# Threshold attention into a maxout FFN: the softmax's 1/sum applied after the product with V instead of before it, with a new issue order

## The chip, the cores and the metric

The kernel runs on one core of one Trainium2 chip. The time is the device time of an execution in microseconds (us); of the kernel before there are three runs.

## The reference

There are 8 batches, 8 heads, 576 positions and a head size of 64. The output has 4608 rows of 512 float32. `randn` inputs stand in float32, tau is 0.02.

```python
scores = scale * np.matmul(q, k.transpose(0, 1, 3, 2))
thresh = np.max(scores, axis=-1, keepdims=True) - tau
scores = np.where(scores >= thresh, scores, -1000000000.0)
scores = scores - np.max(scores, axis=-1, keepdims=True)
attn = np.exp(scores)
attn = attn / (np.sum(attn, axis=-1, keepdims=True) + 1e-09)
x = np.matmul(attn, v)            # then heads side by side: 4608 x 512
h = np.maximum(np.maximum(x @ w1, x @ w2), x @ w3)   # 512 x 768 each
out = h @ w_out                                      # 768 x 512
```

## The kernel before, in words

**Tiling.** A batch has two quads of four heads, so there are 16 quads, `g` = 0 to 15. A quad's attention is cut into nine chunks of 128 partitions (query rows; a partition row holds one query row of one head), each with two halves `r` of 576 columns: 16 x 9 x 2 = 288 halves. Scores come out of float32 matmuls (`sc`) into a PSUM bank. `maximum` (DVE) copies a half to SBUF as `z` and takes its row maximum `nm`. `exponents` (ACT) and `numerators` then make the thresholded exponentials and their sum in one of these ways, chosen per half by a digit of `MASKED`:

- digits 1 and 3 ("masked"): ACT takes Exp, then DVE multiplies by the mask `z >= exp(-tau)` and sums (`SCALAR_TENSOR_TENSOR`);
- digits 0 and 2: ACT applies Prelu with the threshold and then Exp with a sum (two passes on ACT); with 0, DVE makes the threshold `th` first;
- digits 2 and 3 read the scores from PSUM in the first ACT pass instead of from `z`.

`reciprocals` (DVE) takes 1/sum of the two halves of a chunk, `normalized` (POOL) writes `P = z * 1/sum` as bfloat16, half by half, and `turned` sends P through a transposing DMA on SP's queue into `ptq`. When a quad's nine chunks are there, `product` multiplies with V on TensorE (`o`), and the result is evacuated into `xt`, for r = 0 by DVE, for r = 1 by ACT. When both quads of a batch are in `xt`, the FFN follows in pieces: 18 hidden pieces (`ph`; ACT evacuates the first of three, DVE takes the two maxima), then output pieces (`po`). Batch 7 is split in two parts of its rows (`SPLIT`), so there are 18 units of (quad, part) that pass through `product`.

**Order.** Nothing is scheduled at run time. `ORDER` is a string written out by hand or by a planner, one letter for each step, and `issue` carries the letters out; on every engine, and on SP's DMA queue, instructions run in that order. Letters that the text uses: S a half's scores, T transposes of q and k, O a product with V, F and B the two halves of an FFN piece, m maximum, s threshold, e first ACT pass, n second ACT pass, k masked product, r reciprocals, p the scaling on POOL, t the transposing DMA, w and x the evacuation of a product by DVE and by ACT, h and v the evacuations of hidden pieces, l loads of q, k and v, g loads of weights, z their casts on POOL, o and i stores. The digit behind S, T, O, F and N names the pair of PSUM banks, of which there are four.

**Buffers.** Nine z buffers, and from the 72nd half on two more that the weight stage lends (`MORE_Z`, `half_of_z`); six P buffers, two `stage` buffers.

**A reading aid.** All instructions carry the line of one helper (L93), so the profile tells them apart by the names of their tiles.

Of the kernel before, what the change touches and what calls it, by code (L numbers as in the profile page):

```python
# [15 lines left out]
OP = AluOpType  # L16
# [5 lines left out]
FLAT = 2.0 ** -100  # L22

MASKED = """
232222322322222222021032222202332122123122200200111000000000100000000011
000010111020011000101000000001100001001000010011111100000000100100000000
110010030111000100010000000001010100001110001011010100110000000000000000
100101101011000000120000001010000000110011100000001110001000010011111021
# [6 lines left out]
MORE_Z = 72  # L35
# [5 lines left out]
llllllglllT0laclT1laclzllqqS0qqS1meS2mS3lmlT0enlkS1ylmlT2eamelrnpS3leqlmnyS1qcapS0emtnrcS3pmnT2qmepgrelS1qya  # L41
gS0pmelT2mqnS3tcpemqS2nlkT1eytaS0rmnT1kpermS3yS2enczrmS1qT0enmepnqtS3nprmaymgpeS0lptS2mppT0mtpS1enencnqsS3re
rmtpS0mS1penmS3lqnsS2mtperpekzllmT0tmpenkT1pgS3eearnS0petmnqrS2meqlnpS3lmnplsS2cetpremS1pS0nmplermtzeS3mnS2p
mtnpmS3rkpS1leektS0emnrpmemptS1eekS2pO3mktS0rennmpermT2pnS1wptemS3prkyO0tmeakS2pgS1enxlnrmS0lpesS2mezT3mS1np
mgntspcS2eqrseT3mtpeS0srmapS1mnT2ptS3mnqO0ceqmeO1prswnptnkS3pxS0meF1meS2zBresmT0qghF3klpF2nkBtaS1sveS0pemF3B
nyrrsmyBepT1svS0hpcT2nS3zmaS1erpgsF2mntpsBmnS3yvF1etssT0myeBprS2cnpS3mnS0ympelF2epF3lmBnzslssvS0htBrqmeS2vpn
S1gF0sepmF3teqBmF2erssvpBtnBkphF0eS1vtS3znmF2nrBmqteS1rpvBnS3pmlnF0pmgeS1qsBsrhmS3pevS2npS1mF0npsO3ermpesmO2
zewepgsskBxtT3nF1vS2nklBarS0mlphS3mtepF2sS1rmnyBmetF3pvT0eBpcnS2tzT1nvS0asmzS3temS2qeS1meF0trkpmS3lenpBmnlys
reklpF1umerpskS3upBeoketmS0uS2umpS3tesmS1qeT0myO2nqlrsnlprcO3etqsmepwS0xptS1mnF3psnmS2BlerskpS1thF0meF3pmeBF
2ktnBveBsrS1nvpS0hmyF3emF2npBrssT0eprtvBaF1kS3nqvBeF0myhyS2kyleF3mBelBvnpS2snsS0vptemS1pnF3rmpT2tnBmpeF0scS1  # L50
htBrnmpF3erT2rpvlBasS1pstvnS2pmeF0pS3emtBqnmT2S1hcqS3empF2eS0rsqmtS1epsmBeF3pmnF0stsvBeBknF2klhF1BvelS0nrvpB
emT3pS2arvS0ptnS3mpnO1smtesrkpeF2swnlrpmeT0S1qtescS3epBmnpmnT0trskS3paS1umS0ulqmeS3lmyS1nopS2smelS0rmeS3psmn
O1ypersmqO2etkpemO0lewqxlknpS3tS1keF2momS3lexF0ktT1enkBercpnsBpumN1ertkphkF3jS0rursS1empBnmF2ptS0vpS1smeF3yt
BsnsmBpnvS0pT1hmF2atT3srepS0cF1eprBsmeqF3vnByBynvplS2nsS0plmhS1mteS2mF0nF3mteS1rrspBnmS2pelvBlepF1smT0leqBvl
aS2rkhF3oqnsS0mtS1epmBeqsF2ssmtS0epvBeyF1mnF3vpBesrS0ktphBermS1npT2svO0nytmpncT3eS1wF2nrmS0aBrsmnqF3vnT1pS0c
eBptsF2mhpS1eS3pmteS0qmBeO1spmnkteF3rvnpT0BsskapS2xvS0erS1qmtnS3pmnF2mqlespmeS1rtkBepresmT3puS1cuS0ptmnS3pS2
meyS1lrekpF0tnsmempO3lekteskO2nrsmpeBkpxrnwS1uptS3muS2pnmF0yoeS1mF3lesymBtnS2srkpS1hmBeF0spveF2ertBmpT3nrsvS
1paBlmpnS0tS3qhmF1epsmS2leBymF3tevF0nBknlS1rsvpS2esmqnBF3srmhpS1epS0tmeF2pssBrempBtesvS0ynF1mT3lnpBvF0lhsrcS
2tnT1mBnF3valS2nrBsqmeF0pvS1epS2meBptsmS3eqF1hmT2peBcS3tnskT2O0arkplnmO2lerpvewptS3xkpS1nF2meF0sstreBsmpS3nv
pBnmS1tS2hmT3eF0rmpnF1cBpnBrevptT3S2apvS0qmtS3S1enmqF2esrsqmiepmleS0soykeS1plBnmemtS3ukS0uT1snrlO2cpekynO1me  # L60
ymeF3pwxskteS0keS1BrrnkopmF2pmS0BqeuurtsmF1phS3srnpS2meT0ptBmeS3ykpaN2esvempF0tS1jkpF3ermBeS2ptvnS1pmBnS0rls
hsmpS2elF3mqntS1mpF0nsrBskpeF2lsmBetBpveF1yhvS3lnkS2lesF0mytnBmBerqsS3veF2lpvnF1pBsmT0htBceF3rT2vnpBsaS0pvnF
1qmtS2nBsrnmT0pS3hrcpF2esS1mpteS0rmpS3emBpntF1svqnS0ssBmpeoT2vO3lamtneF1wS0nrlBpmeS3qsrS2hsmS0pnmF1eptS3smeB
pmF2ntS0veS3rsmnpS1BnpO0veytrempS2empS3xsmS1tekF0nsknlT2rmpBelmlpnscS3quS1umyS2eorT0kpeO3tmeyO1ewlepsmF3etka
rknS2qklT0nBmxespcS2eryF0mpF1uskpuBtnS2BhmqF3nsvS0peS2srmtpF1eBmpeF0srvnBptS2hyS3pmeF1lmeBlBevtF3nkT2S0arrvp
BnS2mphS1smpF0ntS3smnpBmeF1lsT2esvlF3nrBrcptBnvpS2eS0qmlhS1tsnprsmT3F2epmS0aptBemF3yevS1oS0nqmBnpsrS2mnF1ptv
S0epmBeS3mthS2skeF0F1snmlBeklO3ersvpnrmByepF0swT2eqtBvnqF3ssrcS1hpiBmpT0S2vaptS1snmS0pnT3mqF2tecT1BarmS3pnS1
vqeS0mF2pesrmnptmS3npT1seS0qctBeymqermpS1eS3mpuF0nmtuskS1eS2klnS3smBesrsepO1upmemO2txrkpukeO3wnkpS0xS2emF3et
rmS1pnBssspmF2hS0rtepS3mnBpmF1etS0veF3mnN2rnpBpjF0evtF2esBkBkhF1nsvS3eBmBevO3hrkS2pwnS1mnF3prmS2eptsF0mnBpsS
1sevyS2terBmpeF3svS1iyepBmoS0yhmtF2ekF3nBsmS1ersBvpnF0pmeF2BvteS1hBmF3rsS0vpeF1rknpBBmnO2vhptO0xrpnS3pwS2trm  # L70
npS0mnF3pmteF1pBeBvtS0rS2vpS3empF1ktkF0kBereskpemBkperumO2uptO3xpN1wtenkO2jrF3pxF1hpF2nvF3tvF1rhF2pvF3pvF1hF
2tvF3vF1hF2voF3vF1ohF2vF3vF1hF2vO3vO1wF2xuuF1oF0hiF3vF1vF0hF3vF1vF0hF3vF1vF0hF3vF1vF0hF3vF1vF0huF3vF1ovF3uoF
0uoN1fjdi
# [31 lines left out]
def kernel(  # L105
# [44 lines left out]
    def weight_loads():  # L150


        def piece(dst, src):
            my = {}

            def load():
                my["t"] = stage.tile([128, 4 * 256], F32, name="stage")
# [19 lines left out]
    small = ctx.enter_context(tc.tile_pool(name="small", bufs=6))  # L177
# [177 lines left out]
    halves_of_z = iter(range(1 << 20))  # L355

    def half_of_z():

        n = next(halves_of_z)
        if n >= MORE_Z and (n - MORE_Z) % (ZBUFS + 2) >= ZBUFS:  # L360
            return stage.tile([128, 4 * 256], F32, name="stage")[:, :S]
        return zz.tile([128, S], F32, name="z")

    def maximum(c, r):

        z = c["z", r] = half_of_z()
# [8 lines left out]
    def threshold(c, r):  # L375
        th = c["th", r] = small.tile([128, 1], F32, name="th", bufs=5)
        vector.tensor_scalar(out=th, in0=c["nm", r], scalar1=-1.0, scalar2=tau, op0=OP.mult, op1=OP.subtract)
# [452 lines left out]
```

## Time and profile before

| | |
|---|---|
| median of three runs | 446.92 us (446.69, 446.92, 449.09) |
| profiled execution, span from first to last instruction | 444.8 us; the median lies 2.1 us above it |
| granted TensorE clock, mean | 0.988 |
| DMA | 88.50 MB, 199 GB/s on average |
| scalings `P<-z,rs` and `P<-stage,rs` on POOL | 250 and 38 instructions |
| transposing DMAs `ptq<-P` | 144 |

"Busy" is the time in which an engine has at least one instruction running. Instructions of an engine overlap a little at their ends, so durations add up to more than the busy time. In the tables of windows each row is a stretch of the span, with the busy time of PE (matmuls), PEld (weight loads), DVE, ACT and POOL, then the granted clock, the mean share of the 16 DMA engines that were busy (overlapping packets can bring it over 1) and the rate in GB/s.

### The profile page before, as it was taken

The numbers are of one execution on the slowest core, as the hardware profiler recorded it, in microseconds if no ns is written. First come the engines' busy times: TensorE is split into PE (matmuls) and PEld (weight loads), VectorE is DVE, ScalarE is ACT, GpSimd is POOL, SyncE is SP. The second block draws the span as 40 slices with busy tenths as digits, with TensorE's granted clock in tenths as the row PEclk, the third lists the DMA queues.
The fourth block names the chain that finished last, engine by engine and source line by source line (L and its number), as shares of the span: only waits on it lengthen the run. The fifth ranks groups of instructions, "written<-read, shape, count | busy, mean of one in ns | idle before, by whom it ended". The sixth has DMA issues, their size and how long they took to land.

```text
span 444.8 us, 14254 instructions
## 1 busy us (share of the span) xinstructions
PE 422.4 (95%) x5188; PEld 320.2 (72%) x5190; DVE 392.8 (88%) x1228; ACT 403.0 (91%) x836; POOL 311.9 (70%) x420
## 2 busy tenths in 40 slices
PE   7767789999999999999999999999999999999996
PEld 6334347787788767787788777788688886787873
DVE  3887999999999999999999999998999998899642
ACT  3999999999999999999999999899999999987632
POOL 2799989997878687696785877676676685457400
PEclk8998999999999999999999999999999999999999
DMA  7999999999999999699899999989999977487633
GB/s 188 275 293 199 291 169 269 235 243 262 229 180 194 212 222 292 125 256 167 143 234 189 230 198 203 209 168 210 208 206 194 244 151 105 83 179 136 145 116 108
DMA packets 213959, 88.50 MB, mean 199 GB/s; under 512 B 189184, under 2 KB 202240, under 8 KB 213888
## 3 DMA queue, kind: packets, MB, share of 16 engines
q1 hardware_dynamic: 213360, 86.96, 95.9%
q8 instruction: 41, 0.67, 0.6%
q10 hardware_dynamic: 528, 0.62, 0.5%
q14 instruction: 30, 0.25, 0.2%
HBM read 35.65 MB, written 9.44 MB: 101 GB/s over the span
## 4 chain that ended last, share of the span: by engine, by line
PE 86%; ACT 5%; DVE 4%; issue 2%; DMA 1%; SPq 0%; DVEq 0%; ACTq 0%
PE ph L93 32%; PE sc L93 32%; PE po L93 10%; PE o L93 9%; ACT z L93 5%; PE tp L93 3%; DVE z L93 3%; DMA qm<-in_q_dram 1%; ACT qt L93 1%; SPq L93 0%; DVE xt L93 0%; DVE hm L93 0%; DVE stage L93 0%; DVE rs L93 0%; ACT ob L93 0%
## 5 line engine op out<-in xcount | busy, mean ns | idle before, releaser
L93 POOL TENSOR_SCALAR P<-z,rs 128x576 bf16<-128x576 f32 x250 | 200.6, 814 | 63.3 <-DVE rs L93 28.1
L93 DVE TENSOR_SCALAR_CACHE_REDUCE z<-sc 128x576 f32<-128x576 f32 x250 | 183.7, 750 | 14.8 <-PE sc L93 10.1
L93 PE MATMUL sc<-kt,qs 64*128 64x256 f32 (+2 forms) x640 | 182.6, 423 | 5.7 <-DVE z L93 2.3
L93 PE MATMUL sc<-kt,qt 64*128 64x320 f32 (+2 forms) x640 | 182.4, 433 | 5.2 <-ACT z L93 3.3
L93 PE MATMUL ph<-xt,w 64*128 64x288 bf16 (+2 forms) x2160 | 170.8, 283 | 0.1
L93 PEld LDWEIGHTS <-w 64*128 64x128 bf16 (+1 forms) x2160 | 130.1, 94 | 28.6 <-issue 4.3
L93 ACT ACTIVATE z<-z 128x576 f32<-128x576 f32 x174 | 117.6, 679 | 0.1
L93 PEld LDWEIGHTS sc<-kt,qs 64*128 64x128 f32 (+1 forms) x640 | 92.4, 180 | 25.7 <-DVE z L93 5.7
L93 ACT ACTIVATE z<-z,th 128x576 f32<-128x576 f32 x143 | 106.2, 769 | 5.0 <-DVE th L93 4.2
L93 PEld LDWEIGHTS sc<-kt,qt 64*128 64x128 f32 (+1 forms) x640 | 91.9, 179 | 19.7 <-ACT z L93 5.9
L93 DVE SCALAR_TENSOR_TENSOR z<-z 128x576 f32<-128x576 f32 x76 | 62.2, 830 | 0.5 <-ACT z L93 0.5
L93 PE MATMUL po<-wo,hT 64*128 64x512 bf16 (+3 forms) x454 | 53.5, 354 | 0.3
L93 POOL COPY qs<-qt 64x640 f32<-64x640 f32 (+3 forms) x66 | 43.0, 652 | 10.8 <-ACT qt L93 7.2
L93 ACT ACTIVATE z<-z,nm 128x576 f32<-128x576 f32 x68 | 50.6, 767 | 0.0
L93 DVE TENSOR_TENSOR hm<-ph,hm 128x576 bf16<-128x576 f32 (+2 forms) x54 | 37.0, 686 | 9.2 <-PE ph L93 8.9
L93 ACT ACTIVATE hm<-ph 128x576 bf16<-128x576 f32 (+2 forms) x54 | 31.8, 589 | 13.4 <-PE ph L93 12.8
L93 POOL TENSOR_SCALAR P<-stage,rs 128x576 bf16<-128x576 f32 x38 | 30.4, 804 | 19.3 <-ACT z L93 5.4
L93 PEld LDWEIGHTS <-hT 64*128 64x128 bf16 (+2 forms) x456 | 30.0, 95 | 16.5 <-issue 2.3
L93 DVE TENSOR_TENSOR hT<-ph,hm 128x576 bf16<-128x576 f32 (+2 forms) x54 | 37.0, 686 | 4.0 <-PE ph L93 2.3
L93 PE MATMUL o<-ptq,vb 128*64 128x64 bf16 (+2 forms) x544 | 39.0, 281 | 0.0
L93 ACT ACTIVATION_READ_ACCUMULATOR z<-z 128x1 f32 x174 | 34.3, 197 | 0.0
L93 PEld LDWEIGHTS <-vb 128*64 128x64 bf16 x544 | 23.3, 111 | 12.8 <-issue 4.9
(45 smaller groups left out, 431.6 us busy)
## 6 DMA issues: line engine op xcount, KB each, us to landing
vm<-in_v_dram SPq DMA_DIRECT2D x32, 256.0 KB, 4.8
qm<-in_q_dram SPq DMA_DIRECT2D x15, 512.0 KB, 5.0
km<-in_k_dram SPq DMA_DIRECT2D x15, 512.0 KB, 5.3
out_dram<-ob SPq DMA_DIRECT2D x14, 512.0 KB, 4.0
stage<-in_moe_w_dram SPq DMA_DIRECT2D x9, 512.0 KB, 5.2
ptq<-P SPq DMA_TRANSPOSE x144, 4.0
vr<-in_v_dram SPq DMA_DIRECT2D x16, 128.0 KB, 3.4
stage<-in_moe_w_out_dram SPq DMA_DIRECT2D x3, 512.0 KB, 4.9
```

What stands on the lines that cost most here:

```text
L93: ins = fn(*a, **kw)
```

## The change

P is no longer scaled. `numerators` writes bfloat16 P itself, from ACT's Exp or DVE's masked product, and the sums of a unit's chunks are gathered in one tile `sm` of 20 columns. When a unit's last sum is there, step r takes their reciprocals into `turn` and transposes it in blocks of 32 on DVE; step D (new) stores the result as rows in a DRAM tile; step R (new) loads the rows back with each row spread over 64 partitions, two DMAs for a unit, into a buffer of the weight stage. All evacuations of products are now on DVE and multiply by that tile. POOL's scalings and the letters p and x go; r falls from 144 to 18; D and R come, 18 each. In `MASKED`, 96 halves instead of 86 are masked, 14 instead of 8 of the first 36; no digit 4, which `by_pool` would read, stands in it. `ORDER` is new throughout. The z buffers that the stage lent are given up, and the ninth's output `ob9` uses a z buffer.

```diff
-MORE_Z = 72
...
+    rows = ctx.enter_context(tc.tile_pool(name="rows", bufs=2, space=bass.MemoryType.DRAM))
...
+    def half_of_p(c, r):
+        if "P" not in c:
+            c["P"] = pp.tile([128, W], BF16, name="P")
+        return c["P"][:, r * S:(r + 1) * S]
...
     def numerators(c, r):
-        z, acc = c["z", r], c["sm"][:, r:r + 1]
-        if masked(c["g"], c["idx"], r):
-            vector.scalar_tensor_tensor(out=z, in0=z, scalar=thr, in1=z,
+        z, p, acc = c["z", r], half_of_p(c, r), sum_of(c, r)
...
+        elif masked(c["g"], c["idx"], r):
+            vector.scalar_tensor_tensor(out=p, in0=z, scalar=thr, in1=z,
                                         op0=OP.is_ge, op1=OP.mult, accum_out=acc)
         else:
-            scalar.activation(out=z, in_=z, func=AF.Exp, scale=-1.0 / FLAT, accum_out=acc)
-
-    def reciprocals(c):
-        c["rs"] = small.tile([128, 2], F32, name="rs")
-        vector.reciprocal(c["rs"], c["sm"])
-
-    def normalized(c):
-        c["P"] = P = pp.tile([128, W], BF16, name="P")
-        for n in range(2):
-            pool.tensor_scalar(out=P[:, n * S:(n + 1) * S], in0=c["z", n],
-                                    scalar1=c["rs"][:, n:n + 1], scalar2=1.0, op0=OP.mult, op1=OP.mult)
...
+            scalar.activation(out=p, in_=z, func=AF.Exp, scale=-1.0 / FLAT, accum_out=acc)
...
+    turns = [one.tile([128, 2, 32], F32, name=f"turn{x}") for x in range(2)]
+
+    def reciprocals(g, part, n):
+        L, t = Ls[g], turns[n % 2]
...
+        if part is None:
+            vector.reciprocal(new[:, :, f:f + 9], sums[:, :, f:f + 9])
...
+            vector.reciprocal(new[to, :, at:at + 1], sums[of, :, was:was + 1])
+        vector.transpose(t[:, 1, :], t[:, 0, :])
+        scales[g, part] = dict(t=t)
+
+    def scale_rows(g, part):
+        s = scales[g, part]
+        s["rows"] = rows.tile([32, 128], F32, name="rows")
+        sync.dma_start(out=s["rows"].rearrange("j (b t) -> b j t", b=4), in_=s["t"][:, 1, :])
+
+    def scale_tile(g, part):
+        s, (lo, hi) = scales[g, part], span(part)
+        n = hi - lo
+        s["R"] = stage.tile([128, W], F32, name="stage").rearrange("p (r n) -> p r n", r=2)[:, :, 0:n]
+        src = s["rows"].rearrange("j t -> (j t)")[0:2560].rearrange("(r i y) -> i r y", i=2, y=640)
+        o = 64 * ninth_first(Ls[g]["b"]) + lo
+        for i in range(2):
+            sync.dma_start(out=s["R"][64 * i:64 * i + 64],
+                           in_=src[i, :, o:o + n].unsqueeze(0).to_broadcast([64, 2, n]))
...
-        def on_vector():
...
-            vector.tensor_copy(out=dst[:, lo:hi], in_=ps[:, base:base + hi - lo])
-        def on_scalar():
...
-            scalar.activation(out=dst[:, lo:hi], in_=ps[:, base:base + hi - lo], func=AF.Copy)
+        def done():
+            ps = st["ps"]
+            dst = target(L["b"])[:, 2 * L["qd"] + r, :]
+            vector.tensor_tensor(out=dst[:, lo:hi], in0=ps[:, base:base + hi - lo],
+                                 in1=scales[2 * L["b"] + L["qd"], part]["R"][:, r, :], op=OP.mult)
...
-                ob = hp_.tile([128, DM], F32, name="ob9", bufs=1)
+                ob = zz.tile([128, S], F32, name="z")[:, 0:DM]
```

More of the change, by code (lines that the diff above doesn't have):

```diff
@@ L641 @@
     number = {x: n for n, x in enumerate(steps)}
-    Ls, xts, stores, stores9, ends, ninths = {}, {}, [], [], [], []
+    Ls, xts, stores, stores9, ends, ninths, scales = {}, {}, [], [], [], [], {}
     def x_of(b):
@@ L663 @@
     vector.memset(vrs[2], 0.0)
+    for t in turns:
+        vector.memset(t[:, 0], 1.0)
     for t in vrs[0:2]:
@@ L697, in products, with units @@
                         yield product(Ls[g], r, x_of, part)
+    def units():
+        n = 0
+        for b in range(B):
+            for part in parts_of(b):
+                for g in (2 * b, 2 * b + 1):
+                    yield g, part, n
+                    n += 1
     def flow(what, fn):
@@ L732, in issue @@
             p.first(where)
[L733 to L735 removed]
+            line["w"].append(p.evac)
         elif what in "FN":
@@ L758, in issue @@
             line["k" if masked(c["g"], c["idx"], r) else "n"].append((c, r))
-        elif what in "nk":
-            c, r = line[what].pop(0)
-            if "sm" not in c:
-                c["sm"] = small.tile([128, 2], F32, name="sm")
-            else:
-                c["summed"] = True
-            numerators(c, r)
-        elif what == "r":
-            c = made[line["r"].append(0) or len(line["r"]) - 1]
-            assert c["summed"]
-            reciprocals(c)
-            line["p"].append(c)
+        elif what in "nkX":
+            numerators(*line[what].pop(0))
+        elif what == "r":
+            g, part, n = next(todo["r"])
+            reciprocals(g, part, n)
+            line["D"].append((g, part))
+        elif what == "D":
+            g, part = line["D"].pop(0)
+            scale_rows(g, part)
+            line["R"].append((g, part))
+        elif what == "R":
+            scale_tile(*line["R"].pop(0))
         elif what == "t":
```

154 lines of the change are left out of this document (89 added, 65 removed).

## The prediction

> **What bounds the kernel now.** I read the page's busy table first, then a table of windows, then the groups kept apart by shape, and last the timelines of single engines and of SP's queue.
>
> ```profile
> span 444.8 us, 14254 instructions
> PE 422.4 (95%) x5188; PEld 320.2 (72%) x5190; DVE 392.8 (88%) x1228; ACT 403.0 (91%) x836; POOL 311.9 (70%) x420
> 25.00:50.00 25.00, 18.24 (x128) 10.49 (x128) 20.06 (x63) 23.89 (x54) 24.00 (x33) 0.86 1.13 248
> 50.00:75.00 25.00, 21.51 (x235) 12.67 (x235) 24.84 (x77) 24.75 (x53) 21.96 (x27) 1.00 1.10 232
> 75.00:100.00 25.00, 24.94 (x333) 20.59 (x330) 24.17 (x80) 25.00 (x57) 23.67 (x33) 1.00 1.13 238
> 100.00:125.00 25.00, 25.00 (x308) 19.43 (x309) 23.61 (x75) 24.83 (x51) 20.95 (x27) 1.00 1.13 225
> ```
>
> The columns of the windows are PE, PEld, DVE, ACT, POOL busy, granted clock, DMA share and GB/s. From 75 us on PE is busy for 24.94 and 25.00 of 25 us: from there the kernel is TensorE's, and the change takes no matmul away. Before 75 us PE idles; ACT is full (24.75 of 25) and DVE too (24.84). So a gain can only come from an earlier start of the dense part, and a loss from anything that holes it. The start of the dense part is the first `ph`:
>
> ```profile
> 69.39 1.18 PE L93 MATMUL o<-ptq,vb 128*64 128x512 bf16 x16
> 73.06 0.67 PE L93 MATMUL ph<-xt,w 64*128 64x288 bf16 x8
> 120.36 1.22 PE L93 MATMUL o<-ptq,vb 128*64 128x512 bf16 x15
> 124.10 0.66 PE L93 MATMUL ph<-xt,w 64*128 64x288 bf16 x8
> ```
>
> The product of the second quad of batch 0 runs at 69.39 and the first hidden piece at 73.06; for batch 1 the same pair is at 120.36 and 124.10. Both products need the last transpose of their quad, so SP's queue is the second thing to read.
>
> ```profile
> 56.25 10.68 SPq L93 DMA_TRANSPOSE ptq<-P  x5
> 104.52 1.44 SPq L93 DMA_DIRECT2D vm<-in_v_dram  x2
> 106.00 9.90 SPq L93 DMA_TRANSPOSE ptq<-P  x5
> L93 SPq DMA_TRANSPOSE ptq<-P x144: 1241/1432/4678, 17.6 to 418.9; - x144
> DMA packets 70760, 28.80 MB, mean 230 GB/s; under 512 B 61254, under 2 KB 67398, under 8 KB 70739
> ptq<-P SPq DMA_TRANSPOSE x40, 4.9
> ```
>
> Five transposes fill SP for 10.68 us, five for 9.90 us: 2.1 and 2.0 us each, where the shortest takes 1241 ns. The 28.80 MB row is the window 25:150, the row x40 (4.9 us to landing) the window 50:150. SP has no holes here and the DMA share stands at 1.10 to 1.13: in the first 150 us the queue is as full as ACT. The transposes of batch 1 end at 115.90, landing 4.9 makes 120.8, and the products start at 120.36. Nothing is in reserve there.
>
> **The change part by part.** The rows that price it:
>
> ```profile
> L93 POOL TENSOR_SCALAR P<-z,rs 128x576 bf16<-128x576 f32 x250 | 200.6, 814 | 63.3 <-DVE rs L93 28.1 <-ACT z L93 11.6 <-DVE th L93 7.4
> L93 DVE SCALAR_TENSOR_TENSOR z<-z 128x576 f32<-128x576 f32 x76 | 62.2, 830 | 0.5 <-ACT z L93 0.5
> L93 DVE RECIPROCAL rs<-sm 128x2 f32<-128x2 f32 x144 | 22.0, 157 | 2.0 <-ACT z L93 1.4 <-ACT stage L93 0.2
> L93 DVE TENSOR_TENSOR hm<-ph,hm 128x576 bf16<-128x576 f32 x42 | 31.5, 751 | 0.8 <-PE ph L93 0.6
> L93 DVE CAST xt<-o 128x576 bf16<-128x576 f32 x14 | 10.5, 749 | 0.5 <-PE o L93 0.5
> L93 ACT ACTIVATE xt<-o 128x576 bf16<-128x576 f32 x14 | 9.0, 640 | 0.2
> 402.46 0.67 ACT L93 ACTIVATE z<-z 128x576 f32<-128x576 f32 x1
> 403.12 0.67 ACT L93 ACTIVATE stage<-stage 128x576 f32<-128x576 f32 x1
> 403.79 0.76 ACT L93 ACTIVATE stage<-stage,nm 128x576 f32<-128x576 f32 x1
> 408.27 0.75 DVE L93 SCALAR_TENSOR_TENSOR z<-z 128x576 f32<-128x576 f32 x1
> 408.95 0.75 DVE L93 SCALAR_TENSOR_TENSOR z<-z 128x576 f32<-128x576 f32 x1
> 409.63 0.15 DVE L93 RECIPROCAL rs<-sm 128x2 f32<-128x2 f32 x1
> 409.70 0.13 DVE L93 TENSOR_SCALAR th<-nm 128x1 f32<-128x1 f32 x1
> ```
>
> Durations overlap at their ends, so what an instruction costs its engine is the step from start to start: 0.66 us on ACT (402.46 to 403.12, and 403.12 to 403.79), 0.68 on DVE for a full half (408.27 to 408.95), 0.07 for a small one (409.63 to 409.70).
>
> *POOL.* All 288 scalings go: 200.6 us of this form alone. In the windows POOL is full only from 25 to 50 (24.00 of 25), and ACT is as full there, so this frees latency (a P is ready one or two passes of 0.81 us sooner) and no bound by itself.
>
> *ACT.* The masks hold 96 masked halves instead of 86: ten exponentials fewer, 10 x 0.66 = 6.6 us. The evacuations of x leave: 14 x 0.640 = 9.0, and four small ones. About 16 us of 403.0.
>
> *DVE.* 144 reciprocals go, 144 x 0.07 = 10 us; 18 groups of two to four reciprocals and a transpose of 128x32 come. That transpose has no row: between a small instruction (0.07) and a full half (0.68); with so few elements I take 0.15, so 18 x 0.35 = 6 us. Ten masked halves more: 10 x 0.68 = 6.8. Evacuations of x: 14 x 0.749 = 10.5, and four small ones, 12 us in all; the multiplication costs nothing over the cast by the row of `hm<-ph,hm` (751 against 749). On the other side, the masked product takes 830 ns on average, but 0.75 at 408.27 and 408.95, where POOL ran nothing; without POOL's scalings the 96 save up to 0.08 each, 7.7 us. Balance about +7 us on 392.8. The Trainium skill says why, in "SBUF — State Buffer", section "Who interferes with whom": a VectorE instruction with two SBUF inputs contends with a GpSimd instruction that reads SBUF. By that rule the 7.7 us come in full, and the rows agree.
>
> *The front.* Counted in the two orders up to the first hidden piece, before to after: Prelu or Exp of the first pass 50 to 47, second-pass exponentials 37 to 29, masked products 12 to 16, maxima 53 to 52, evacuations of x on ACT 2 to 0, on DVE 2 to 4. With the steps above and the evacuations of the transposes, ACT's work falls from 62.7 to 54.7 us, DVE's goes from 54.8 to 56.4. The larger falls by 6.3 us. That is what the change can win, if the data come in time.
>
> *SP and the DMAs.* Each of 18 units adds a store of 16 KB (D), and two loads that spread 295 KB each over 64 partitions (R). R must wait on SP until D has landed; behind it on SP stand transposes, loads and stores. The new evacuation waits on DVE for R; behind it stand maxima, masked products and the maxima of the hidden pieces, and PE waits for those to free banks.
>
> ```profile
> qm<-in_q_dram SPq DMA_DIRECT2D x15, 512.0 KB, 5.0
> out_dram<-ob SPq DMA_DIRECT2D x3, 64.0 KB, 2.6
> 77.42 1.34 SPq L93 DMA_TRANSPOSE ptq<-P  x1
> 78.85 0.56 SPq L93 DMA_DIRECT2D stage<-in_moe_w_dram  x1
> 79.46 0.65 SPq L93 DMA_DIRECT2D vm<-in_v_dram  x1
> ```
>
> D is nearest to the 64 KB store (2.6 us to landing), R to the 512 KB load (5.0). A plain DMA holds SP for 0.56 to 0.65 us, say 0.6. Now batch 1, where nothing is in reserve. The old queue reaches the end of its 36th transpose at 115.90. The new one must reach the fourth R; counted in the order, that is one transpose more, two loads more, four D and eight R issues: 2.0 + 14 x 0.6 = 10.4 us. By bytes it is 0.295 + 0.6 + 8 x 0.295 = 3.26 MB, at 230 GB/s 14.2 us. The bounds are 0 (transposes fall back to 1241 ns: 37 x 0.76 us is more than all that is added) and 14.2; I take 10.4, since five in a row took 2.0 each even with few loads among them. Against it stands the front's relief: P comes earlier by at most 6.3 us, and I credit all of it. Net 4.1 us. R's landing (5.0) replaces the transpose's (4.9). So the hidden pieces of batch 1 start near 128 instead of 124.10, and as PE was dense from 75 us on, nothing gives that back.
>
> The Trainium skill speaks against this detour in "DMA: Bandwidth & Descriptors", sections "Anatomy of one DMA" and "Two DMAs through the same engine are not ordered": a DMA has a fixed cost of about 2.0 us, mostly the receipt of its write, heaviest for HBM, and a dependent DMA must wait on the issuing engine for the first one's semaphore. The 2.6 us row agrees; by the page D would cost 0.6 us less than I take.
>
> *The tail.* In the new order the seventeenth R has one masked product (0.68) between it and the evacuation that waits for it, and the eighteenth nothing. DVE then waits up to 5.0 - 0.7 = 4.3 us with hidden maxima queued behind.
>
> ```profile
> 415.09 8.03 PE L93 MATMUL ph<-xt,w 128*128 128x256 bf16 x72
> ```
>
> Eighteen hidden pieces of the first part (72 matmuls) take PE 8.03 us, 0.45 each. After the seventeenth R PE has in hand two products, a ninth and two hidden pieces, some 3.0 us; DVE's wait outlasts them by 1.3 us. At the eighteenth the cover is two products and an output chunk, and how far SP is by then I cannot read; between 0 and 5.0 us, I take 0.4, since the hidden pieces before it last 8 us and the last masked product lies early in them. Together 1.7 us, bounds 0 and 9.3.
>
> *At no cost.* The halves of z that stood in the stage's buffers go back to nine: z is now free when its numerator is read, without POOL's pass, and the seat before that is what the two extra ones held. The ninth's output moves into z's pool at a time when few halves are live. If this cover is missing, a maximum waits for a z, one step of 0.68 us each time. P is now held from its first numerator on; with six of them and a queue 4 us later, numerators can wait for a transpose to land. That is how the queue's delay reaches ACT and DVE, and it is in the 4.1 already.
>
> **Sum.** Span 444.8 + 4.1 + 1.7 = 450.6 us. The median of the runs, 446.92, lies 2.1 us above the profiled span; the same put on top gives 452.7 us, 1.3% slower.
>
> **Rivals.**
> *The front wins (faster).* If the large rows of R flow beside the transposes, because it is the small packets (61254 of 70760 under 512 B) that are slow, then the queue does not bind and the first hidden piece starts when DVE's 56.4 us are done instead of ACT's 62.7: 6.3 us earlier, and the dense part moves with it. 446.9 - 6.3 = 440.6, with half of the tail 441.5 us. For it: ACT is at 24.75 of 25 before the first hidden piece, and the loads of weights stand later in the new order. Against it: SP without holes and 2.0 us a transpose. It decides where the fourth R lands before the old queue's 120.8.
> *Nothing to be measured.* The relief and the queue cancel: 10.4 becomes about 6, and the tail is covered. Then PE starts its dense part where it did, and nothing else counts: 447 us.
> *The queue stays full to the end (much slower).* R's wait for D blocks SP. In the order six units have no other transfer between D and R and six have one; that is 6 x 2.6 + 6 x about 1.2 = 23 us in which SP stands, beside 18 x 1.8 = 32 us of issues. Of a batch's 51 us (73.06 to 124.10) SP then needs 18 x 2.0 + 14 x 0.6 for the old work, 3.6 for issues and 2.6 for waits: 50.6. The backlog is never worked off, and each of the five batches behind the second, by my estimate, loses 1 to 2 us more: 452.7 + 7 = 460 us. For it: the DMA share is over 1 in the 300 to 325 window too; against it: GB/s there is lower than in the first 150 us, so transposes should cost less than 2.0.
>
> ```profile
> 300.00:325.00 25.00, 25.00 (x312) 18.64 (x307) 23.34 (x76) 24.64 (x52) 16.41 (x24) 1.00 1.09 214
> ```
>
> *It does not do what it says.* A mask digit for a POOL path exists in the code, but no mask uses it; the exponentials and products change by ten. If DVE's products stay at 830 without POOL, DVE has 14 us more than before instead of 7, and at 24.84 of 25 in the front 1 to 2 us show: inside the range.
>
> **Chances.** The forecast's case 0.45, the front wins 0.22, nothing to be measured 0.11, the queue full to the end 0.22. About 0.5% is what a measurement of this kernel can tell from no change (its three runs differ by that much), so 444.7 to 449.2 is "same". Faster 0.22, same 0.11, slower 0.67. The range must leave out at most 0.2: it reaches from the front's case, 441, past the full queue's 460 to 464, for the byte bound of 14.2 is 3.8 us above what I took. The forecast's own range is 448 to 458.
>
> **What would show it.** Right: the second quad's products of batch 1 still near 120, but the first hidden piece of batch 1 near 128; before it the new evacuation on DVE waiting for the DMA of R by several us, and PE holes of some us between 75 and 150, where there are none now; ACT near 387 busy, DVE near 400, POOL near 80; the masked products near 750 ns. Wrong: the first hidden piece of all before 70 us and no waits for R on DVE (the front wins), or holes of PE of like size in every batch up to 400 us (the full queue). The queue step is wrong if R lands within 3 us, or if transposes in the first 150 us fall to 1.3 us each. Above all the prediction fails if the DMAs have room that the 1.10 to 1.13 does not show.

## The result, and the profile after

The changed kernel takes 497.62 us, the median of four runs (495.69 to 500.42), against 447.05 us (446.69 to 449.09) for the kernel before: a ratio of 1.1133, 95% interval 1.1084 to 1.1182. The forecast was 452.7 us, with a range of 441 to 464. The direction is right; the time lies 34 us above the range. An execution can fall into a slower state; of e4 and e5 below one run each did, and their times are those of the other three.

The profiled execution of the changed kernel, the page's busy rows, packets, reads and the chain that ended last:

```profile
span 494.8 us, 13734 instructions
...
PE 435.9 (88%) x5188; PEld 320.7 (65%) x5190; DVE 403.9 (82%) x1180; ACT 390.4 (79%) x798; POOL 89.0 (18%) x132
...
DMA packets 221514, 98.19 MB, mean 198 GB/s; under 512 B 192136, under 2 KB 206216, under 8 KB 221448
...
HBM read 45.09 MB, written 9.73 MB: 111 GB/s over the span
...
PE 48%; DMA 18%; DVE 17%; ACT 8%; issue 6%; SPq 2%; DVEq 0%; ACTq 0%
```

All engines do about the work that was forecast, but the span is 50.0 us longer. It splits in two from the busy rows alone: TensorE idles for 494.8 - 435.9 = 58.9 us instead of 444.8 - 422.4 = 22.4, which is 36.5 us; and the same 5188 matmuls keep it busy 13.5 us longer. DMA is 18% of the chain. The same windows as before the change, with the same columns:

```profile
25.00:50.00 25.00, 14.55 (x112) 8.90 (x108) 21.74 (x61) 21.05 (x45) 9.43 (x11) 0.85 1.07 226
50.00:75.00 25.00, 21.50 (x200) 13.80 (x200) 17.78 (x55) 17.89 (x39) 5.79 (x9) 0.88 1.01 218
75.00:100.00 25.00, 22.02 (x270) 16.75 (x272) 21.13 (x62) 19.59 (x41) 8.98 (x12) 0.86 1.09 241
100.00:125.00 25.00, 22.43 (x266) 17.18 (x268) 20.17 (x60) 20.54 (x44) 4.64 (x7) 0.93 0.97 227
300.00:325.00 25.00, 18.69 (x238) 14.91 (x235) 16.23 (x48) 17.59 (x34) 2.98 (x3) 1.00 1.13 230
```

No engine is full now, not even in the window at 300, where PE had 25.00 of 25. The DMAs are about as busy as before: their share lies between 0.97 and 1.13, where it was 1.09 to 1.13, and over the whole run they move 198 GB/s instead of 199, but 98.19 MB instead of 88.50. In the table below, read from PE's timelines, the delay is followed from batch to batch by the start of the first hidden piece (us):

| | batch 0 | 1 | 2 | 3 | 4 | 5 | 6 | end |
|---|---|---|---|---|---|---|---|---|
| before | 73.1 | 124.1 | 171.1 | 224.8 | 273.0 | 325.7 | 374.6 | 444.8 |
| after | 79.0 | 140.5 | 194.2 | 255.4 | 309.7 | 368.4 | 423.3 | 494.8 |
| later by | 5.9 | 16.4 | 23.1 | 30.6 | 36.7 | 42.7 | 48.7 | 50.0 |

Each of the batches 0 to 6 loses 6 to 10.5 us; what follows the last of these pieces loses 1.3. How a batch loses them is seen at the first one. The timelines of SP's queue, of DVE and of PE:

```profile
57.17 7.07 SPq L89 DMA_TRANSPOSE ptq<-P  x4
64.34 0.60 SPq L89 DMA_DIRECT2D rows<-turn  x1
65.00 1.33 SPq L89 DMA_DIRECT2D vm<-in_v_dram  x2
66.38 0.61 SPq L89 DMA_DIRECT2D q<-in_q_dram  x1
67.09 0.44 SPq L89 DMA_DIRECT2D stage<-in_moe_w_dram  x1
67.64 1.60 SPq L89 DMA_DIRECT2D stage<-rows  x2
69.29 1.47 SPq L89 DMA_DIRECT2D k<-in_k_dram  x1
70.80 0.51 SPq L89 DMA_DIRECT2D qm<-in_q_dram  x1
75.96 0.37 SPq L89 DMA_DIRECT2D stage<-in_moe_w_dram  x1
```

```profile
70.79 0.08 DVE L89 DVE_READ_ACCUMULATOR z<-sc 128x1 f32 x1
77.07 0.76 DVE L89 TENSOR_TENSOR xt<-o,stage 128x576 bf16<-128x576 f32 x1 [6.20 <-DMA stage<-rows]
```

```profile
69.71 1.18 PE L89 MATMUL o<-ptq,vb 128*64 128x512 bf16 x16
...
71.93 0.38 PE L89 MATMUL sc<-kt,qs 64*128 64x256 f32 x1
77.97 0.76 PE L89 MATMUL sc<-kt,qs 64*128 64x256 f32 x1 [5.67 <-DVE th L89]
...
78.96 4.83 PE L89 MATMUL ph<-xt,w 64*128 64x288 bf16 x39
```

The product of the second quad starts at 67.62 and 69.71, where before it stood at 69.39: it is no later. But R (`stage<-rows`) is issued at 67.64 and has landed only when the evacuation starts at 77.07. DVE waits 6.20 us for it, PE idles behind DVE, and the first hidden piece starts at 78.96 instead of 73.06. The tile R shares the DMAs with what was issued around it. In batch 1 the chain is longer still: reciprocals at 122.4, D on SP at 128.0, R at 132.2, the evacuation at 138.98. SP gets to D and to R late, since transposes and loads stand ahead of both.

What a hole costs does not end with the hole. The windows around this one:

```profile
72.00:78.00 6.00, 0.33 (x6) 0.06 (x2) 0.93 (x3) 0.08 (x1) 1.04 (x1) 0.89 0.85 181
78.00:85.00 7.00, 7.00 (x68) 5.04 (x68) 5.20 (x15) 4.74 (x8) 1.04 (x1) 0.61 1.07 284
```

After 6 us with PE idle the granted clock is 0.61 for the next 7 us, with PE busy throughout. Up to the last matmul the clock stands at 0.5 for stretches that add up to 40.8 us in this execution, and to 10.2 us before; PE is busy in 31.3 us of the first and in 10.1 us of the second. The Trainium skill describes this in "TensorE: Matmul & The Clock Gate", section "Part 1: The HAM clock gate": an idle window of about 3.4 us halves the clock until TensorE has again been busy for such a window. The trace agrees for the four longest holes of PE (5.3 to 7.6 us): 6.8 us at half clock go with each. It does not agree throughout: 3.4 us at half clock also follow two holes of 2.5 and 2.4 us, and 6.8 us begin at 28.9 with no hole over 1.5 us ahead of them. A score matmul of 64x320 takes 0.74 us at half clock (at 78.67) and 0.43 at the full one (at 83.62). If all work takes up to twice as long there, the 21.2 us of busy time added at half clock make, by this estimate, up to 10.6 of the 13.5 us by which PE's busy time grew; the rest stays open.

Two rows of the waits name what DVE waited for (us in total, times, longest us):

```profile
DVE xt L89 <- DMA stage<-rows: 28.5, 9, 6.2
...
DVE z L89 <- DMA out_dram<-z: 13.2, 2, 7.7
```

The first is the forecast wait for R. The second is the ninth's store: a maximum waits for the z buffer from which the ninth's output is still to be stored, twice, for 13.2 us in all. The forecast had that move at no cost.

### The profile page after: what moved, and what is told of

It reads as the page before. It is cut to its first block, busy times and chain, and to the rows that moved or that the text cites. A ratio compares the mean times of both kernels' runs of the same rounds, so it can differ in the third digit from the quotient of the medians.

```text
span 494.8 us, 13734 instructions
## 1 busy us (share of the span) xinstructions
PE 435.9 (88%) x5188; PEld 320.7 (65%) x5190; DVE 403.9 (82%) x1180; ACT 390.4 (79%) x798; POOL 89.0 (18%) x132
## 2 busy tenths in 40 slices
DMA packets 221514, 98.19 MB, mean 198 GB/s; under 512 B 192136, under 2 KB 206216, under 8 KB 221448
## 3 DMA queue, kind: packets, MB, share of 16 engines
HBM read 45.09 MB, written 9.73 MB: 111 GB/s over the span
## 4 chain that ended last, share of the span: by engine, by line
PE 48%; DMA 18%; DVE 17%; ACT 8%; issue 6%; SPq 2%; DVEq 0%; ACTq 0%
PE ph L89 21%; PE sc L89 16%; DMA stage<-rows 9%; DVE z L89 8%; PE po L89 5%; ACT z L89 4%; DMA rows<-turn 4%; PE o L89 3%; PE tp L89 2%; ACT P L89 2%; SPq L89 2%; DMA out_dram<-z 2%; DMA ptq<-P 2%; DVE P L89 2%; DVE hT L89 2%
## 5 line engine op out<-in xcount | busy, mean ns | idle before, releaser
L89 DVE TENSOR_SCALAR_CACHE_REDUCE z<-sc 128x576 f32<-128x576 f32 x288 | 209.3, 751 | 29.1 <-PE sc L89 14.4
L89 ACT ACTIVATE z<-z,th 128x576 f32<-128x576 f32 x171 | 127.4, 767 | 13.4 <-DVE th L89 13.4
L89 ACT ACTIVATE P<-z 128x576 bf16<-128x576 f32 x192 | 129.2, 675 | 1.6 <-DMA ptq<-P 1.1
L89 PEld LDWEIGHTS sc<-kt,qs 64*128 64x128 f32 (+1 forms) x640 | 96.1, 184 | 33.7 <-issue 13.2
L89 PEld LDWEIGHTS sc<-kt,qt 64*128 64x128 f32 (+1 forms) x640 | 96.5, 183 | 26.9 <-DVE z L89 6.3
L89 POOL COPY qs<-qt 64x640 f32<-64x640 f32 (+3 forms) x66 | 46.6, 706 | 230.6 <-ACT qt L89 196.5
L89 DVE SCALAR_TENSOR_TENSOR P<-z 128x576 bf16<-128x576 f32 x96 | 75.4, 790 | 0.2
L89 ACT ACTIVATE z<-z,nm 128x576 f32<-128x576 f32 x88 | 66.1, 766 | 0.0
L89 ACT ACTIVATE hm<-ph 128x576 bf16<-128x576 f32 (+2 forms) x54 | 31.9, 591 | 42.7 <-PE ph L89 42.7
L89 DVE TENSOR_TENSOR xt<-o,stage 128x576 bf16<-128x576 f32 (+2 forms) x36 | 24.2, 686 | 32.7 <-DMA stage<-rows 28.5
L89 ACT ACTIVATION_READ_ACCUMULATOR P<-z 128x1 f32 x192 | 37.1, 193 | 0.0
L89 ACT ACTIVATE qt<-tp 128x640 f32<-128x640 f32 (+3 forms) x34 | 21.0, 617 | 18.5 <-PE tp L89 14.2
L89 PEld LDWEIGHTS <-vb 128*64 128x64 bf16 x544 | 23.1, 111 | 14.8 <-issue 6.7
## 6 DMA issues: line engine op xcount, KB each, us to landing
vr<-in_v_dram SPq DMA_DIRECT2D x16, 128.0 KB, 3.3
```

Of the source, the lines that this page charges most:

```text
L89: ins = fn(*a, **kw)
```

## The experiments

Four causes were set against each other. *The waits*: DVE stands for R, and what is queued behind it stands too. *The bytes*: R adds 9.4 MB to DMAs that are full already (HBM reads 45.09 MB against 35.65), so all transfers come later, whoever waits. *The ninth*: its output holds a z buffer until SP has stored it. *The order*: the new `ORDER` itself is worse. Where one time is given it is one run; the runs of kernels timed more often lie up to 5 us from their median, so a step below 5 us that rests on a single run is not told from scatter.

### The waits, and the ninth in another buffer

e1 puts the ninth's output into the two buffers of the ordinary output pieces:

```diff
-                ob = zz.tile([128, S], F32, name="z")[:, 0:DM]
+                ob = hp_.tile([128, 2, DM], F32, name="ob")[:, 0]
```

> Edit: the ninth's output goes into the output pool's own buffer again instead of a z buffer; all else as changed. Theory W (waits: DVE stands for a z that the ninth's store still holds, and for R; each hole also halves TensorE's clock for a while): the two waits of 5.5 and 7.7 us go, and with them two stretches of 6.8 us at half clock that cost up to 3.4 us each, so 497.6 falls by 13 to 20 us, to 478 to 484. Theory Q (queue: SP and the DMAs are full, so that transposes are late whatever else waits): the delay moves to the next transpose, 490 to 497. Theory O (the new order and masks by themselves are worse): little change, 490 or more.

Measured: 494.98 us. The wait moved rather than went: it is ACT now that waits for an output buffer, in the second of these rows of the waits.

```profile
DVE xt L89 <- DMA stage<-rows: 25.0, 7, 6.5
...
ACT ob L89 <- DMA out_dram<-ob: 18.3, 4, 8.9
```

A shared pool is not a buffer of its own; this run could not price the ninth.

e2 issues D and R as the change does, but evacuates without them:

```diff
-            vector.tensor_tensor(out=dst[:, lo:hi], in0=ps[:, base:base + hi - lo],
-                                 in1=scales[2 * L["b"] + L["qd"], part]["R"][:, r, :], op=OP.mult)
+            vector.tensor_copy(out=dst[:, lo:hi], in_=ps[:, base:base + hi - lo])
```

> Edit: D and R are issued as in the changed kernel, but the evacuation copies the product without multiplying, so it does not wait for R (the division by the sum is left out). SP's queue and the DMAs carry the same work. Theory W: the 28.5 us of waits on R go, and about 6 us of half clock, so about 463. Theory Q: transposes stay late, 485 to 497. Theory O: 485 to 497.

Measured: 494.84 us, 2.8 below the change. All 28.5 us of waits for R are gone and the time stays. By its waits, DVE and PE now stand elsewhere:

```profile
DVE z L89 <- DMA out_dram<-z: 21.6, 3, 12.3
...
PE tp L89 <- DMA km<-in_k_dram: 10.4, 3, 4.6
...
PE tp L89 <- DMA qm<-in_q_dram: 9.8, 3, 5.8
```

The transposes of the next q and k wait for their loads. So taking the wait for R away wins nothing here: the loss moves to other waits.

e3 is e1 without D and R (no `scale_rows`, no `scale_tile`, a plain copy).

> Edit: no D and no R at all, evacuation without multiplying (the division by the sum is left out), and the ninth in its own buffer; masks and order as changed. What is left is the order, the masks and P written by ACT and DVE. Theory W: all waits gone, 441 to 447, since ACT and DVE have less to do up to the first hidden piece. Theory Q: the same, 441 to 450. Theory O: 455 or more.

Measured: 469.36 us, 25.6 us below e1. D and R are worth about half of the loss, and 22 us remain without them. Only *the order* had put e3 this high (455 or more).

### Another queue

e4 has the full computation, with e1's ninth, and issues D and R from POOL's queue, where nothing stands ahead of them:

```diff
-        sync.dma_start(out=s["rows"].rearrange("j (b t) -> b j t", b=4), in_=s["t"][:, 1, :])
+        pool.dma_start(out=s["rows"].rearrange("j (b t) -> b j t", b=4), in_=s["t"][:, 1, :])
...
-            sync.dma_start(out=s["R"][64 * i:64 * i + 64],
+            pool.dma_start(out=s["R"][64 * i:64 * i + 64],
```

> Edit: D and R are issued from POOL's queue, which the change left nearly idle, instead of SP's, and the ninth has its own buffer; the result is the full one. D no longer stands behind transposes, and SP no longer stands for D. Theory W: from the end of the sums to R's landing it should take D's and R's landings alone, some 8 us, most waits on DVE go, 450 to 462. Theory Q: the DMAs carry the same bytes, so no better than the first experiment of this set, 475 to 484. Theory O: 475 or more.

Measured: 495.73 us (493.44 to 500.35), ratio 1.1057 (1.1016 to 1.1098). SP is relieved of 54 issues and of D's round trip, and nothing is won over e1 (494.98). By its waits, DVE stands for R as long as in the change, and POOL's queue holds R back until D has landed:

```profile
POOL stage L89 <- DMA rows<-turn: 38.4, 15, 4.9
...
DVE xt L89 <- DMA stage<-rows: 28.2, 8, 7.8
```

POOL's standing is not what eats the gain: by their waits, the other engines stand for POOL for 0.4 us in all. So SP's time, the term from which the forecast was made, is worth nearly nothing by this run. The time lies above what the waits (450 to 462) and the queue (475 to 484) gave; the order is tried next.

### The order

e5 is the change with the order and the masks of before, converted: p dropped, x made w, r and D where a unit's last r stood, R behind a unit's last t. e6 is e5 without D and R and with a plain copy.

```diff
-llllllT0lT1lcaqlqaS2cqqS0mS3lemS1mS2lneeT3mmaeqcT0aS1lcqqS3mmlnlS0sllelS1mS2eellmmeT2kqT3eS1aykS2nskS0mlmene
+llllllglllT0laclT1laclzllqqS0qqS1meS2mS3lmlT0enlkS1ylmlT2eamelnS3leqlmnyS1qcaS0emtncS3mnT2qmegelS1qyagS0melT
...
```

> Edit: the change with the order and the masks of before. The old order string is kept letter for letter, except that p goes, x becomes w, the reciprocals of a unit stand where those of its last chunk stood, D follows them at once and R follows the unit's last transpose. Theory Q (the bytes and issues of D and R are what is too much for SP and the DMAs): near the changed kernel, 480 to 500. Theory O (the new order itself costs what the third experiment left, some 20 us, because its loads and transposes come at worse places): 465 to 475. If both are wrong and the new scheme only needed this order, 441 to 455.

> Edit: as the fifth, but without D and R, evacuation by a copy (the division by the sum is left out). What is left is P written by ACT and DVE and all evacuations on DVE, in the old order with the old masks. Theory O: 441 to 449, like before or better, since POOL's pass and ten per cent of nothing else is gone; the 469 of the third experiment is then the new order's. If 460 or more, then it is P or z that is short (six P, nine z, held longer), and not the order.

Measured: e5 493.61 us (491.96 to 495.46), ratio 1.1048 (1.0997 to 1.1099); e6 467.85 us. With the old order the change costs what it costs with the new one, and D and R again some 26 us of it. The order is not the cause. What e3 and e6 still share is the reciprocals on DVE and a ninth in a pool that others use; e8 below takes both away.

### Bytes against waits

e7 leaves all D, R, waits and issues in place but loads only 32 columns of each row, 16 KB instead of 288 KB, and multiplies the whole row by the first of them:

```diff
-                           in_=src[i, :, o:o + n].unsqueeze(0).to_broadcast([64, 2, n]))
+                           in_=src[i, :, o:o + 32].unsqueeze(0).to_broadcast([64, 2, 32]))
```

> Edit: the changed kernel with R cut from 576 to 32 columns of a row (16 KB instead of 295 KB a DMA); the evacuation multiplies by the first column, a scalar for each partition, so it still waits for R and takes as long (the division is wrong by that). Issues, waits and order stay; 10 MB go. Theory Q by bytes: most of the 26 us between the first and the third experiment go, 470 to 478. Theory Q by issues and by R's wait for D on SP: 488 to 498.

Measured: 477.22 us, 20.4 below the change. e8 has no r, D or R at all, a plain copy, a buffer of the ninth's own, and 1024 columns of stage again:

```diff
-                ob = zz.tile([128, S], F32, name="z")[:, 0:DM]
+                ob = hp_.tile([128, DM], F32, name="ob9", bufs=1)
...
-            reciprocals(g, part, n)
```

> Edit: as the third (no D, no R, evacuation by a copy, the division left out), without the reciprocals too, and with a buffer for the ninth that nothing else uses (the stage goes back to 1024 columns to make room). In the third experiment the ninth waited for an output buffer instead (ACT stood 16 us for the store). If that wait was real loss, 469 falls by 8 to 14 us, to 455 to 461; if transposes or loads are late anyway, it stays at 465 to 470.

Measured: 449.18 us. Its busy row:

```profile
PE 421.3 (94%) x5188; PEld 314.8 (70%) x5190; DVE 395.8 (89%) x1124; ACT 389.1 (87%) x798; POOL 90.2 (20%) x132
```

This is below both answers that were offered. The new order and the unscaled P, with no scaling at all, are 2 us behind the kernel before, which a single run does not tell from nothing. The 222 us that POOL and the 14 us that ACT are spared here buy nothing.

### The ninth stored at once

e9 is the change with the ninth's store issued by ACT right behind the evacuation, instead of by SP when the order comes to it:

```diff
-                def store():
-                    for x in range(2):
-                        sync.dma_start(out=out[(b + x - 1) * S:(b + x) * S, :].rearrange("(p c) m -> p c m", c=9)[:, 8],
-                                       in_=ob[64 * x:64 * x + 64])
-                stores9.append(store)
+                for x in range(2):
+                    scalar.dma_start(out=out[(b + x - 1) * S:(b + x) * S, :].rearrange("(p c) m -> p c m", c=9)[:, 8],
+                                     in_=ob[64 * x:64 * x + 64])
```

e10 is e9 with e7's small rows, e11 is e9 with no D and R but with the reciprocals, e12 is e9 with e2's plain copy.

> Edit: the changed kernel, but the ninth's store is issued from ACT right behind the evacuation that fills its z buffer, instead of later from SP; the result is the full one. Theory A (two causes that add: the ninth's buffer some 20 us, as between the third experiment's 469 and the eighth's 449, and D and R some 26 us): 475 to 480. Theory B (not additive: while D and R fill SP and the DMAs, something else is late where the ninth was): 488 to 497.

> Edit: the ninth's store at once from ACT, and R cut to 32 columns as in the seventh (the scaling is wrong by that). Issues of D and R and the waits for them stay. Theory A: the seventh's 477 less the ninth's 20 us, 455 to 460. Theory B: 468 or more.

> Edit: the ninth's store at once from ACT, no D and no R, evacuation by a copy (the division by the sum is left out). It differs from the eighth only in how the ninth gets out of the way and in keeping the reciprocals. Both theories: 447 to 453; if it is 460 or more, the store at once does not free the z buffer in time and the ninth experiment says nothing on the ninth.

> Edit: the ninth's store at once from ACT; D and R are issued in full, but the evacuation copies and does not wait for R (the division by the sum is left out). Theory A with the bytes as the price: as the ninth experiment, 472 to 480. Theory A with the waits of DVE for R as the price: 449 to 458. Theory B: 485 or more.

Measured: e9 490.32 us (488.35 to 491.69), ratio 1.0962 (1.092 to 1.1004); e10 466.37; e11 461.01; e12 486.13. The earlier store takes 7.3 us off the change. e9 and e12 lie where the causes were said not to add up (488 to 497, and 485 or more), e10 between its two answers. Cutting R's bytes takes 23.9 us off e9; not waiting for R takes 4.2, which is within the scatter. e9 and e10 issue the same DMAs; the page's packet row of the two, e9 first:

```profile
DMA packets 221514, 98.19 MB, mean 201 GB/s; under 512 B 192136, under 2 KB 206216, under 8 KB 221448
```

```profile
DMA packets 221514, 89.35 MB, mean 193 GB/s; under 512 B 196744, under 2 KB 209800, under 8 KB 221448
```

As many packets, 8.84 MB less: it is bytes that cost 23.9 us, not the number of packets, not the round trip of D and R. e12 shows how: nothing waits for R there, and it still takes 25.1 us more than e11, which issues neither D nor R (some 5 of them go to these issues by e10 against e11). PE, ACT and DVE stand 46.6 us for other loads, stores and transposes in e12, and 14.6 us in e11. R's bytes delay the other transfers. e11 missed what was expected of it (447 to 453), and above 460 it left open whether e9 says anything on the ninth. Between it and e8 12 us were open; the last three runs go after those.

### Reciprocals, the ninth alone, half the bytes

e13 is e11 without r, e14 is e13 with the ninth stored late by SP as in the change. e15 is e9, the full computation, with the rows in bfloat16, half of R's bytes:

```diff
+        low = small.tile([128, 32], BF16, name="low", bufs=2)
+        vector.tensor_copy(out=low, in_=t[:, 1, :])
...
-        s["rows"] = rows.tile([32, 128], F32, name="rows")
+        s["rows"] = rows.tile([32, 128], BF16, name="rows")
```

> The changed kernel with the ninth stored by ACT at once, and without the steps r, D and R altogether: the product is evacuated by a plain copy (the scaling is left out). The run with r kept took 461.0 us, the one with nothing of the three, the ninth in a buffer of its own and its store late on SP took 449.2. If the reciprocals and the transpose on DVE make those 12 us (they end each unit, and PE waits for hidden maxima behind them): 449 to 452. If the ninth does (a slot of z held until ACT's store has landed, and the issue on ACT): 458 to 461.

> The same without r, D and R, but the ninth stored late by SP, as the change has it, from its slot of z. Against the run with a buffer of its own (449.2 us) only the ninth's place differs, and the two columns of the weight stage. If the slot of z has a price of its own, whatever D and R do: 456 to 460. If it is dear only where SP is late by the bytes of R: 449 to 452.

> The changed kernel with the ninth stored at once and the rows of 1/sum in bfloat16 (a copy of 128x32 more on DVE in each unit): as many DMAs and packets as before, half of R's bytes. With all bytes it took 490.3 us, with 32 columns of each row 466.4. If the bytes are what R costs, in proportion: 479 (476 to 482). If it is the number of packets, the round trip of D and R, or a threshold: near 490 or near 467.

Measured: e13 453.49 us (451.81 to 454.49), ratio 1.0135 (1.0081 to 1.019); e14 469.88 (467.88 to 472.76), ratio 1.051 (1.0444 to 1.0577); e15 472.90 (472.12 to 474.37), ratio 1.0581 (1.0518 to 1.0643).

e13 lies between the two answers that were offered: r is worth 7.5 us (461.01 to 453.49) and the ninth's z, stored at once, some 4. For r the busy rows agree, 403.4 us of DVE in e11 (first) against 395.3 here:

```profile
PE 427.5 (93%) x5188; PEld 317.0 (69%) x5190; DVE 403.4 (88%) x1180; ACT 390.0 (85%) x798; POOL 88.3 (19%) x132
...
PE 420.0 (93%) x5188; PEld 313.3 (69%) x5190; DVE 395.3 (87%) x1126; ACT 388.9 (86%) x798; POOL 90.5 (20%) x132
```

e14 shows that the late store from z has a price of its own, 16.4 us over e13 and more than the 456 to 460 us offered, with no R in the kernel at all. Against e13 the first hidden piece falls back by 5.5 us up to batch 3, by 6.7 more up to batch 5 and by 3.4 more up to batch 7: once for each ninth that two batches share. The row of the waits says the same:

```profile
DVE z L89 <- DMA out_dram<-z: 16.0, 3, 6.9
```

One of the three, from the timelines of ACT, of SP's queue and of DVE in e14:

```profile
289.23 0.60 ACT L89 ACTIVATE z<-po 128x512 f32<-128x512 f32 x1 [1.23 <-PE po L89]
```

```profile
289.87 2.05 SPq L89 DMA_TRANSPOSE ptq<-P  x1
292.29 0.63 SPq L89 DMA_DIRECT2D out_dram<-ob  x1
293.02 0.53 SPq L89 DMA_DIRECT2D km<-in_k_dram  x1
293.67 2.01 SPq L89 DMA_TRANSPOSE ptq<-P  x1
295.73 0.88 SPq L89 DMA_DIRECT2D out_dram<-ob  x1
296.66 1.38 SPq L89 DMA_DIRECT2D out_dram<-z  x2
```

```profile
295.87 0.08 DVE L89 DVE_READ_ACCUMULATOR z<-sc 128x1 f32 x1
302.89 0.76 DVE L89 TENSOR_SCALAR_CACHE_REDUCE z<-sc 128x576 f32<-128x576 f32 x1 [6.94 <-DMA out_dram<-z]
```

The ninth is in z at 289.8. Its store stands behind two transposes, two output stores and a load until 296.66, and lands before 302.89. The buffers are handed out in turn, and the sixth maximum that starts after the evacuation began gets this one: it waits 6.94 us, and all of DVE's queue with it.

e15 misses all its answers and tells that the price of the bytes is not in proportion. From e10 to e15 the kernel moves 3.98 MB more (89.35 to 93.33) and loses 6.5 us (466.4 to 472.9); from e15 to e9 it moves 4.86 MB more and loses 17.4 us (472.9 to 490.3). That is 1.6 us and 3.6 us a MB. The row of DVE's waits for R, of e15 and then of e9:

```profile
DVE xt L89 <- DMA stage<-rows: 11.7, 5, 5.7
```

```profile
DVE xt L89 <- DMA stage<-rows: 29.6, 10, 6.7
```

DVE waits for R 5 times instead of 10, and by the DMA issues of the two R lands 3.0 us after its issue (median) instead of 4.6. So about the first half of R's bytes is cheap and the rest dear; why is not shown.

### The ledger

| step | us | against the line above |
|---|---|---|
| new order, P unscaled, no r, D or R, the ninth alone (e8) | 449.2 | +2.1 (the kernel before) |
| the ninth in z, stored at once (e13) | 453.5 | +4.3 |
| r on DVE (e11) | 461.0 | +7.5 |
| D and R with few bytes (e10) | 466.4 | +5.4 |
| R's bytes up to half (e15) | 472.9 | +6.5 |
| the other half (e9) | 490.3 | +17.4 |
| the ninth stored late (after) | 497.6 | +7.3 |

The steps depend on the path: the late store costs 16.4 us where there is no R, 7.3 with R, which fits delays by R that cover part of it. e8, e10 and e11 are single runs, so the steps of 2.1 and 4.3 are within the scatter and that of 5.4 is barely outside. No version with the scaling in it comes near the kernel before; the best one with the full computation, e15, is 5.8% slower.

## Why the prediction was wrong

**The step that failed** is the sum under "SP and the DMAs". It had the cause right in the main (the DMAs of the first 150 us have little room) and priced it in the wrong unit and over the wrong stretch. The unit was SP's time: 14 issues of 0.6 us and one transpose, 10.4 us. It rests on the reading that SP has no holes and that a transpose takes 2.0 us. SP's own waits in the kernel before, from 25 to 150 us, say otherwise:

```profile
SPq L93 <- POOL P L93: 33.8, 25, 3.5
```

SP stands 33.8 us for POOL's P there, in 25 waits. Waits of SP stand inside the records of its DMAs: in the group of five transposes at 56.25 one takes 4.36 us and the other four 1.28 to 1.50, and the median of all 144 is 1.43. (In the group at 106.00 two of 2.69 and 2.04 us show no wait, so part of the 2.0 was real.) And e4 takes D and R off SP and gains nothing; e10 and e9 differ in bytes alone and by 23.9 us. The stretch: bytes were counted only up to the fourth R, 14.2 us as the upper bound for batch 1, and nothing was added for the batches behind it. Yet each batch brings two more units, and the table of first hidden pieces grows by 6 to 10.5 us in every one. The bound that the prediction's own row of 230 GB/s gave for the whole run, 9.4 MB / 230 GB/s = 41 us, was not worked out; the bytes' 23.9 us lie within it.

The rival **"the queue stays full to the end"** named the right shape and was mis-sized: 1 to 2 us a batch, where 6 to 10.5 were measured. Its 23 us in which SP stands for D are about what SP's waits show (20.1 us in 12), but e4 tells that they are not the price. It took the lower GB/s at 300 us as room; by e15 the room is good for about half of R's bytes.

**"At no cost"** was wrong for the ninth. It said that the cover, if missing, would cost one step of 0.68 us each time. A z buffer held by a store is missing until SP has come to the store and it has landed: 16.0 us in three waits in e14. What the sentence lacked was the queue ahead of the store on SP.

**DVE behind the front.** The balance of DVE was worked out and then given no term in the sum. In r it holds a cost: 8.1 us of DVE (e11 against e13), and 7.5 us of the kernel's time.

**Holes and the clock.** No term stood for the half clock that goes with a hole. Of the 50.0 us 13.5 are PE's longer busy time, and up to 10.6 of these, by the estimate above, the half clock.

**Batch 1**: "near 128" for its first hidden piece; 140.5 was measured, already 5.9 us late from batch 0, where the prediction looked only at SP and not at R's landing. R was expected 5.0 us after its issue; the median is 4.4, but in the chain that ended last the two units that matter take 8.35 us (batch 0) and 5.98 (batch 1), and their evacuations start 9.4 and 6.8 us behind R's first issue. D was expected at 2.6 us; where it stands in the chain, six times, it takes 2.04 to 4.85. The 2.0 us of the Trainium skill that the prediction sets beside it stand in a section on DMAs that GpSimd issues ("DMA: Bandwidth & Descriptors", "Anatomy of one DMA"), and D is issued by SP; the measurement decides. D's wait on SP behind transposes (5.0 us in batch 1) had no term.

**The front**: it does win when nothing follows it: the first hidden piece starts at 70.6 in e13 and 70.7 in e8, against 73.1. That is 2.5 us of the 6.3 credited, and by batch 1 it is gone (128.7 and 127.7 against 124.1).

**Right**: the tail, 1.7 forecast, 1.3 measured (71.5 us from the first hidden piece of batch 6 to the end, 70.2 before), and DVE waits 3.7 us for the seventeenth R where up to 4.3 was expected; that the two small holes add up so closely is partly luck, since the second was a guess between 0 and 5.0. DVE's balance, 403.9 us for 400; ACT's, 390.4 for 387; POOL's, 89.0 for 80. Under DVE, two terms were off: the transpose takes 211 ns for the 150 assumed, and the masked product fell to 790 ns, not 750. The groups kept apart by shape:

```profile
L89 DVE SCALAR_TENSOR_TENSOR P<-z 128x576 bf16<-128x576 f32 x96 | 75.4, 790 | 0.2
...
L89 DVE TENSOR_TENSOR xt<-o,stage 128x576 bf16<-128x576 f32 x28 | 20.8, 753 | 26.3 <-DMA stage<-rows 24.8 <-PE ph L89 1.3 <-PE o L89 0.2
...
L89 DVE STREAM_TRANSPOSE turn<-turn 128x32 f32<-128x32 f32 x18 | 3.8, 211 | 0.6
```

The multiplication at the evacuation is free on DVE, as forecast: 753 ns against the cast's 749. The masked products thus gave 96 x 40 ns = 3.8 us of the 7.7. The rule of the Trainium skill in "SBUF — State Buffer", section "Who interferes with whom", would give all of it only if POOL read nothing; it still runs 89 us of copies and casts.

**Open**: why e10's D and R, with few bytes, still cost some 5 us (single runs), how r's 8.1 us on DVE become 7.5 us of time, and why the second half of R's bytes costs more than the first; e15 shows the bend, not its cause. The DMAs' mean rate is no fixed ceiling either: e13 and e14 move the same 88.45 MB at 196 and 190 GB/s.

## What to carry to other kernels

Where the DMA share stands at 1, work out the bytes of an added transfer over the whole run at the rate of those windows as the bound of its price (here 41 us, of which 23.9 came), and not the issue time of its queue at one place. Spreading one row over 64 partitions by DMA costs the bytes of 64 rows: look for the factor in the shape before all else. A buffer moved into a busy pool is held until its store lands; so count what stands ahead of that store on its queue, and compare with the time in which the pool comes round.

## What was not expected of the hardware

- A hole of 6 us in PE costs up to 3 us more, by estimate: the clock is at half from 76.6 us, within the hole, for 6.8 us (0.61 on average from 78 to 85 us), and PE works in 5.5 of these.
- The same 221514 packets with 8.84 MB less take 23.9 us off the kernel; 4.86 MB less take off 17.4 already.
- The queue that issues a DMA made no difference (SP 495.0 in e1, POOL 495.7 in e4) where the DMA share stands near 1.
